# A decode-attention kernel that streams its caches: one load queue against two that take turns

## The chip, the cores and the metric

The kernel runs on one core of one Trainium2 chip. The metric is the device time of one execution in microseconds (us), the median over runs of the same kernel; lower is better.

## The reference

One token attends over two key/value caches of 8192 positions, and the two results are mixed by a gate. Block A has 16 heads with a cache each; block B has 16 query heads on 8 cached heads. Everything is float32, and a head has 256 numbers.

```python
def block(x, k_cache, v_cache, wq, wo, rep):            # A: rep 1, B: rep 2
    q = (x @ wq).reshape(1, 1, 16, 256).transpose(0, 2, 1, 3)
    k, v = repeat(k_cache, rep, axis=1), repeat(v_cache, rep, axis=1)
    p = softmax(einsum("bhqd,bhkd->bhqk", q, k) / 16)
    return einsum("bhqk,bhkd->bhqd", p, v).transpose(0, 2, 1, 3).reshape(1, 1, 4096) @ wo

g = sigmoid((x * gate_w).sum(-1, keepdims=True))
out = g * block(x, A_k, A_v, A_wq, A_wo, 1) + (1 - g) * block(x, B_k, B_v, B_wq, B_wo, 2)
```

## The kernel before, in words

All that is read (both caches, both wq and wo, x and the gate's weights) lies in one array, `stream`, in the order of use. The program works through 8 sets. A set has three units: two B heads that share a cache (unit 2), then A heads 0 and 1. A unit has 4 key tiles and 4 value tiles of 2 MB (128 partitions x 4096 numbers), so that a set has 12 of each; a value tile stands 3 tiles behind its key tile (`LEAD`).

`plan()` cuts the stream into `LOADS`, 54 **fills**, which I count from 0. Fills 0 to 50 hold 15872 numbers a partition (7936 KB; fill 0 has 8 more) and are one load each: almost four tiles, cut without regard to the tiles' ends. Fill 0 holds x, the gate's weights, the first wq and key tiles 0 to 2. Fills 51, 52 and 53 are cut into 2, 3 and 7 loads for the end of the program. That makes 63 loads.

Fills go in turn into the 3 slots of the pool `ring` (`SLOTS`). The loop at L464 takes a slot for the next fill, issues its loads on SyncE's queue (L469), and calls `piece` for each part of the fill (L472), which writes out the work on it. SyncE has nothing else to do: a load waits there until the engines are done with the fill that had the slot, three fills earlier, and then goes out.

What the work on a fill is, by lines:

- A key tile of unit 2 or of head 1 goes through `scores`: 16 matmuls on TensorE (L255), a minimum on VectorE (L261, L262), an exponential on ScalarE with its sum read by an accumulator read (L264), and a transpose on VectorE (L267).
- A key tile of head 0 goes through `scores_by_row` on VectorE: a multiply in place (L277) and a sum (L281) over the whole tile, some small steps, an exponential on ScalarE (L290) and a multiply (L294).
- A value tile goes through `attend`: 16 matmuls (L307). At a unit's end `take` (L316 on ScalarE, L317 on VectorE) copies the sum out, and `gather`, `combine` (L345 on ScalarE), `column` and `project_o` make the weights of the unit.
- wq goes through `project` (L220) and `spread`, wo through `emit_set` (L381) and, for the last set, `emit` (L398).

The order on each engine is the order in which the program is written (`manual_schedule`); the framework adds the waits.

Of the kernel before, what the change touches and what calls it, by code (L numbers as in the profile page):

```python
# [14 lines left out]
P = 128  # L15
# [18 lines left out]
SLOTS = 3  # L34
# [12 lines left out]
def plan():  # L47

    size = {"xg": XG, "k": ROWS * DH, "v": ROWS * DH, "wq": WQ, "wo": 8 * D}
    per = len(UNITS) * NT  # L50
    n = len(TILES)
    items = []
    for i in range(n + LEAD):
        if i == 0:
            items += [("xg", 0), ("wq", 0)]
        if i < n:
            items.append(("k", i))
        if i >= LEAD:
            items.append(("v", i - LEAD))
        if i % per == 7 and i // per + 1 < NS:  # L60
            items.append(("wq", i // per + 1))
        if i % per == LEAD + 1 and i >= per:
            items.append(("wo", i // per - 1))
    loads, room = [[]], FULL
    last = [("v", n - 3), ("v", n - 2)]
    for kind, i in items[:items.index(last[0])]:
        at, left = 0, size[kind]
        while left:
            step = min(left, room) // ATOM[kind] * ATOM[kind]
            if step:  # L70
                loads[-1].append((kind, i, at, step))
            at, left, room = at + step, left - step, room - step * (kind != "xg")
            if left:
                loads.append([])
                room = FULL

    loads = [[x] for x in loads]
    x = loads[-2][0]
    loads[-2] = [x[:2], x[2:]]
    loads[-1] += [[(kind, i, 0, size[kind])] for kind, i in last]  # L80
    at, end = 0, []
    for c in LAST_CUT:
        end.append([("v", n - 1, at, c * DH)])
        at += c * DH

    for h, e, n in ((3, 0, 2), (0, 0, 2), (1, 0, 3), (2, 1, 1)):
        end.append([("wo", NS - 1, (2 * h + e) * D, n * D)])
    return loads + [end]


LOADS = plan()
# [3 lines left out]
def kernel(  # L95
# [5 lines left out]
    nc = tc.nc  # L101
# [89 lines left out]
    def inputs(xs):  # L191
        nc.vector.tensor_copy(xz[:, :KF, 0], xs[:, :KF])
        nc.vector.tensor_copy(xz[:KR, KF, 0:1], xs[:KR, KF:])  # L193
        nc.vector.tensor_copy(xz[KR:, KF + 1, 0:1], xs[KR:, KF:])

    def prepare(gw):
        clear(YY[0], D)
        gp = ps_s.tile([1, 1], F32, name="sm")
        for c in range(KF + 1):
            nc.tensor.matmul(gp, xz[:, c, 0:1], gw[:, c:c + 1], start=(c == 0), stop=(c == KF))  # L200
        ge = const.tile([1, 1], F32, name="ge")
        nc.scalar.activation(ge, gp, AF.Exp, scale=-1.0)
        nc.vector.tensor_scalar(ge, ge, 1.0, None, op0=OP.add)
        nc.vector.reciprocal(gate[:, 0:1], ge)
        nc.vector.tensor_scalar(gate[:, 1:2], gate[:, 0:1], -1.0, 1.0, op0=OP.mult, op1=OP.add)
# [5 lines left out]
    def project(s, c0, w):  # L211

        if c0 == 0:
            QR[s] = ps_s.tile([2 * BLK, 2 * DH], F32, name="sm")
        q = QR[s]
        for j in range(w.shape[1]):
            a, c = divmod(c0 + j, KF)
            for a in (a,) if a < 2 else (0, 1):
                c = c if c0 + j < 2 * KF else KF
                nc.tensor.matmul(q[BLK * a:BLK * (a + 1), :], xz[:, c if c < KF else KF + a, :], w[:, j, :],  # L220
                                 start=(c == 0), stop=(c == KF), skip_group_check=True)
        if c0 + w.shape[1] == 2 * KF + 1:
            QR[s] = small.tile([P, NB * BLK], F32, name="px")[:2 * BLK, :2 * DH]
            nc.scalar.activation(QR[s], q, AF.Copy)

    def spread(s):

        qt = ps_s.tile([P, 2, 2, 2], F32, name="sm")
        qr = QR.pop(s)
        for h in range(2):  # L230
            for e in range(2):
                at = h * DH + e * P
                nc.tensor.matmul(qt[:, h, e, :], qr[:, at:at + P], rows4[:2 * BLK, :2], start=True, stop=True)
        for r, a, h, M in ((2, 0, 0, 2), (0, 1, 0, 1), (1, 1, 1, 1)):
            if (s, r) in BY_ROW:
                qa = ps_s.tile([P, DH], F32, name="sm")
                nc.tensor.matmul(qa, spread32, qr[:, h * DH:(h + 1) * DH], start=True, stop=True)  # L237
                QA[s, r] = small.tile([P, DH], F32, name="qa", bufs=1)
                nc.scalar.activation(QA[s, r], qa, AF.Copy, scale=-scale)
                continue  # L240
            nc.vector.tensor_scalar(QB[s % 2, r][:, :, BLK:BLK + M], qt[:, h:h + M, :, a].rearrange("p h e -> p e h"),
                                    -scale, None, op0=OP.mult)
# [76 lines left out]
    def gather(u):  # L319

        M = heads(u)
        GS[u] = small.tile([P, 2, NG, NT, M], F32, name=f"gs{M}")
        if u in BY_ROW:
            nc.vector.tensor_tensor(GS[u][:, :, :, :, 0], ST[u][:, :, None, :].to_broadcast([P, 2, NG, NT]),
                                    in4[:, :, :, None].to_broadcast([P, 2, NG, NT]), op=OP.mult)
            return
        pos = POS[M].rearrange("p g (t m) -> p g t m", m=M)
        for k in range(2):
            nc.vector.tensor_tensor(GS[u][:, k], ST[u][:, k, None, :, None].to_broadcast([P, NG, NT, M]), pos, op=OP.mult)
# [76 lines left out]
    def wait(n, f, *args):  # L406
        todo.append([n, f, args])

    def tick():
        for t in todo:  # L410
            t[0] -= 1
        for t in [t for t in todo if t[0] <= 0]:
            todo.remove(t)
            t[1](*t[2])

    def piece(kind, i, at, view):
        n = view.shape[-1] // ATOM[kind]
        j0 = at // ATOM[kind]
        if kind == "xg":
            inputs(view[:, :KF + 1])  # L420
            GW[0] = view[:, KF + 1:]
        elif kind == "wq":
            project(i, j0, view.rearrange("p (c n) -> p c n", c=n))
            if j0 + n < 2 * KF + 1:
                pass
            elif i == 0:
                spread(0)
                prepare(GW[0])
            else:
                wait(1, spread, i)  # L430
        elif kind == "k":
            u, t = TILES[i]
            if u in BY_ROW:
                scores_by_row(u, t, 2 * j0, view.rearrange("p (j d) -> p j d", d=DH))
            else:
                scores(u, t, j0, view.rearrange("p (c n) -> p c n", c=n))
            if j0 + n < 2 * NG:
                return
            tick()
            if t == NT - 1:  # L440
                gather(u)
                wait(1, combine, u)
                wait(2, column, u)
        elif kind == "v":
            u, t = TILES[i]
            n = view.shape[-1] // DH
            attend(u, t, at // DH, n, view.rearrange("p (j d) -> p j d", d=DH))
            if at // DH + n == ROWS:
                if t == NT - 1:
                    take(u)  # L450
                    if u != TILES[-1][0]:
                        wait(1, project_o, u)
                if i >= len(TILES) - LEAD:
                    tick()
        elif kind == "wo" and i < NS - 1:
            emit_set(i, j0, view.rearrange("p (c n) -> p c n", c=n))
            if i == NS - 2 and j0 + n == 8:
                fold()
        else:
            for j in range(n):  # L460
                LAST[divmod(j0 + j, 2)] = view[:, j * D:(j + 1) * D]

    off = 0
    for fill in LOADS:  # L464
        buf = ring.tile([P, FULL + XG], F32, name="slot")
        c = 0
        for load in fill:
            n = sum(x[3] for x in load)
            nc.sync.dma_start(buf[:, c:c + n], stream[off:off + P * n].rearrange("(p n) -> p n", p=P))  # L469
            off += P * n  # L470
            for x in load:
                piece(*x[:3], buf[:, c:c + x[3]])  # L472
                c += x[3]
    assert not todo
    s = NS - 1
    project_o((s, 1))
# [75 lines left out]
```

## Time and profile before

| | |
|---|---|
| median of 3 runs | 1010.63 us (1010.38 to 1011.29) |
| the profiled execution | 1010.95 us, span 1009.2 us |
| moved from memory | 432.02 MB, mean 429 GB/s over the span |
| busy share of the span: TensorE, VectorE, ScalarE | 57%, 46%, 9% |
| the loads' queue: share of the 16 DMA engines' span | 99.1% |
| granted TensorE clock, mean | 0.773 |

The profile is of one execution. Its span runs from the first instruction to the last; the execution's own time is 1.75 us longer than that. Busy time is the time in which an engine executes; a DMA engine's is the time that its packets took. For each idle stretch of an engine the profile names what ended it.

### The profile page before, as it was taken

The page shows a single profiled execution, that of the slowest core. Times are in us where ns is not written, and L with a number is a line of the kernel's source. Part 1 is how long each engine was busy: PE and PEld are TensorE (multiplying, and loading weights), DVE is VectorE, ACT ScalarE, POOL GpSimd, SP SyncE. Part 2 cuts the span into 40 slices and gives each one's busy share as a digit, 9 for nine tenths or more (in the row PEclk, how much of TensorE's full clock was granted, in tenths as well). Part 3 has the DMA queues.
Part 4 walks back from the last instruction along what each step waited for, and adds up shares of the span by engine and source line. Part 5 has one row for each costly group of instructions (what it writes and reads, how often), then busy time and mean ns, then how long its engine had stood idle before and what let it go on. Part 6 is the DMA issues. An engine that isn't in the chain of part 4 may idle for free.

```text
span 1009.2 us, 7624 instructions
## 1 busy us (share of the span) xinstructions
PE 578.0 (57%) x3154; PEld 169.8 (17%) x3154; DVE 465.1 (46%) x732; ACT 90.0 (9%) x267; POOL 1.9 (0%) x10
## 2 busy tenths in 40 slices
PE   0846745565745655636646556645656537537557
PEld 0211211121211111112111111111211112111112
DVE  1486213961248521576215841248521585216851
ACT  0100100010100110001100001100110000101010
POOL 0000000000000000000000000000000000000000
PEclk9977877767777887867787777776886777777788
DMA  9999999999999999999999999999999999999997
GB/s 403 439 438 425 431 436 439 435 421 433 439 436 425 436 431 441 431 428 433 441 428 429 438 431 433 435 431 438 431 431 426 440 438 426 428 433 441 424 421 299
DMA packets 9114, 432.50 MB, mean 429 GB/s; under 512 B 1016, under 2 KB 1144, under 8 KB 1784
## 3 DMA queue, kind: packets, MB, share of 16 engines
q1 hardware_dynamic: 9080, 432.02, 99.1%
q8 instruction: 24, 0.39, 0.2%
q14 instruction: 10, 0.08, 0.0%
HBM read 432.02 MB, written 0.00 MB: 428 GB/s over the span
## 4 chain that ended last, share of the span: by engine, by line
DMA 71%; PE 14%; DVE 12%; ACT 2%; issue 1%; ACTq 0%; SPq 0%; DVEq 0%
DMA slot<-in_stream_dram 71%; PE o L307 6%; PE sc L255 5%; DVE sr L281 4%; DVE slot L277 4%; PE sm L220 2%; ACT px L264 1%; DVE mn L261 1%; DVE pr L267 1%; PE sm L237 0%; DVE pr L294 0%; ACT pxr L290 0%; ACT ew L345 0%; PE sm L361 0%; DVE st L262 0%
## 5 line engine op out<-in xcount | busy, mean ns | idle before, releaser
L307 PE MATMUL o<-slot,pr 128*32 128x512 f32 (+1 forms) x1536 | 349.9, 758 | 224.6 <-DMA slot<-in_stream_dram 224.6
L255 PE MATMUL sc<-slot,qb 128*32 128x512 f32 x1024 | 197.5, 715 | 104.7 <-DMA slot<-in_stream_dram 101.7
L261 DVE TENSOR_REDUCE mn<-sc 128x1 f32<-128x512 f32 x64 | 44.1, 690 | 325.7 <-PE sc L255 300.9
L277 DVE TENSOR_TENSOR slot<-slot,qa 128x4096 f32<-128x4096 f32 (+7 forms) x40 | 142.6, 3565 | 41.1 <-DMA slot<-in_stream_dram 41.0
L307 PEld LDWEIGHTS o<-slot,pr 128*32 128x32 f32 (+1 forms) x1536 | 80.0, 142 | 405.2 <-DMA slot<-in_stream_dram 252.8
L281 DVE TENSOR_REDUCE sr<-slot 128x16 f32<-128x4096 f32 (+7 forms) x40 | 142.7, 3567 | 1.4
L255 PEld LDWEIGHTS sc<-slot,qb 128*32 128x32 f32 x1024 | 46.3, 129 | 221.1 <-issue 126.1
L264 ACT ACTIVATE px<-sc,st 128x512 f32<-128x512 f32 x64 | 44.0, 687 | 408.5 <-DVE st L262 386.6
L267 DVE STREAM_TRANSPOSE pr<-px 128x512 f32<-128x512 f32 x64 | 45.6, 713 | 58.9 <-ACT px L264 58.9
L220 PE MATMUL sm<-slot,xz 128*32 128x512 f32 x128 | 45.7, 707 | 35.8 <-DVE xz L193 23.0
L290 ACT ACTIVATE pxr<-sr,st 128x16 f32<-128x16 f32 x32 | 9.8, 308 | 373.6 <-DVE st L288 373.6
L372 PE MATMUL sm<-sel,ob 128*128 128x1 f32 (+1 forms) x96 | 17.5, 287 | 37.3 <-DVE ob L317 37.3
L317 DVE SCALAR_TENSOR_TENSOR ob<-o,half,ob 128x256 f32<-128x256 f32 x24 | 11.3, 470 | 44.0 <-ACT ob L316 44.0
L372 PEld LDWEIGHTS sm<-sel,ob 128*128 128x128 f32 x96 | 15.5, 228 | 61.8 <-DVE ob L317 53.6
L220 PEld LDWEIGHTS sm<-slot,xz 128*32 128x32 f32 x128 | 11.1, 128 | 65.4 <-issue 27.8
L294 DVE TENSOR_TENSOR pr<-pxr,cols 128x256 f32<-128x256 f32 x32 | 13.6, 426 | 15.9 <-ACT pxr L290 15.9
L316 ACT ACTIVATE ob<-o,half 128x256 f32<-128x256 f32 x24 | 11.3, 469 | 49.5 <-PE o L307 49.5
L361 PE MATMUL sm<-ones,wr 1*128 1x1 f32 x48 | 9.7, 268 | 10.4 <-DVE wr L354 10.4
L237 PE MATMUL sm<-px,spread 64*128 64x256 f32 x16 | 6.6, 498 | 13.9 <-DVE es L347 13.9
L381 PE MATMUL Y<-slot,ocs 128*1 128x448 f32 x112 | 13.4, 595 | 0.0
L361 PEld LDWEIGHTS sm<-ones,wr 1*128 1x128 f32 x48 | 7.8, 203 | 32.8 <-issue 28.1
L264 ACT ACTIVATION_READ_ACCUMULATOR px<-sc,st 128x1 f32 x64 | 12.3, 193 | 0.0
(73 smaller groups left out, 142.4 us busy)
## 6 DMA issues: line engine op xcount, KB each, us to landing
slot<-in_stream_dram SPq DMA_DIRECT2D x50, 7936.0 KB, 42.6
slot<-in_stream_dram SPq DMA_DIRECT2D x1, 7940.0 KB, 22.0
slot<-in_stream_dram SPq DMA_DIRECT2D x1, 4864.0 KB, 41.0
slot<-in_stream_dram SPq DMA_DIRECT2D x2, 2048.0 KB, 25.3
slot<-in_stream_dram SPq DMA_DIRECT2D x1, 3072.0 KB, 29.9
slot<-in_stream_dram SPq DMA_DIRECT2D x1, 1280.0 KB, 20.8
slot<-in_stream_dram SPq DMA_DIRECT2D x1, 1024.0 KB, 24.2
slot<-in_stream_dram SPq DMA_DIRECT2D x2, 512.0 KB, 25.5
```

The source lines that it names most:

```text
L220: nc.tensor.matmul(q[BLK * a:BLK * (a + 1), :], xz[:, c if c < KF else KF + a, :], w[:, j, :], start=(c == 0), stop=(c == KF), skip_group_ ...
L255: nc.tensor.matmul(sc[32 * g:32 * (g + 1), :], qb[:, e, at:at + 32], kt[:, j, :], start=(e == 0), stop=(e == 1), skip_group_check=True)
L261: nc.vector.tensor_reduce(mn, sc, axis=AX.X, op=OP.min)
L264: nc.scalar.activation(px, sc, AF.Exp, bias=st[:, 0, t:t + 1], scale=-1.0, accum_out=st[:, 1, t:t + 1])
L267: nc.vector.transpose(pr.rearrange("p (q r k) -> p q k r", r=BLK, k=2), px.rearrange("p (q k c) -> p q k c", c=BLK, k=2))
L277: nc.vector.tensor_tensor(kt, kt, QA[u][:, None, :].to_broadcast([P, n, DH]), op=OP.mult)
L281: nc.vector.tensor_reduce(sc[:, j0:j0 + n], kt, axis=AX.X, op=OP.add)
L294: nc.vector.tensor_tensor(pr, px[:, :, None, :].to_broadcast([P, ROWS // 2, NG * NT, 2]), cols[:, t].rearrange("p g r -> p (g r)")[:, None ...
L307: nc.tensor.matmul(O[u][w * g:w * (g + 1), :], pr[:, j // 2, :w], vt[:, j - j0:j - j0 + 2, :], start=(t == 0 and j < 2 * P // w), stop=(t ...
L361: nc.tensor.matmul(cl, WR.pop(u).rearrange("p c x m k -> p (c x m k)"), ones[:1, :], start=True, stop=True)
L372: nc.tensor.matmul(oc[:, e, :M], OB[u][:, e::2], SEL[u][:, :M], start=True, stop=True)
L381: nc.tensor.matmul(YY[0][32 * h:32 * h + 1, :], OC[s, r][:, e, m:m + 1], wt[:, j, :], start=False, stop=(s == NS - 2 and e == 1), skip_gro ...
```

## The change

The loads are taken out of the loop into `ask(k)`, which takes the slot for fill k and issues its loads. Fills with an even number go out on SyncE's queue, fills with an odd one on ScalarE's; the last three all go out on SyncE's. The first three fills are asked for ahead of the loop. In the loop, fill k + 3 is asked for behind the work on fill k. On SyncE that is the place that it had. On ScalarE, whose instructions run in the order in which they are written, the load now stands among the exponentials and copies: behind all that ScalarE has to do for fill k.

```diff
-    off = 0
-    for fill in LOADS:
+    off = [0]
+    queues = [nc.sync, nc.scalar]
+
+    def ask(k):
         buf = ring.tile([P, FULL + XG], F32, name="slot")
         c = 0
+        for load in LOADS[k]:
+            n = sum(x[3] for x in load)
+
+            queue = queues[k % 2 if k < len(LOADS) - 3 else 0]
+            queue.dma_start(buf[:, c:c + n], stream[off[0]:off[0] + P * n].rearrange("(p n) -> p n", p=P))
+            off[0] += P * n
+            c += n
+        return buf
+
+    bufs = [ask(k) for k in range(SLOTS)]
+    for k, fill in enumerate(LOADS):
+        c = 0
         for load in fill:
-            n = sum(x[3] for x in load)
-            nc.sync.dma_start(buf[:, c:c + n], stream[off:off + P * n].rearrange("(p n) -> p n", p=P))
-            off += P * n
             for x in load:
-                piece(*x[:3], buf[:, c:c + x[3]])
+                piece(*x[:3], bufs[k][:, c:c + x[3]])
                 c += x[3]
+        if k + SLOTS < len(LOADS):
+            bufs.append(ask(k + SLOTS))
```

On ScalarE, at the program's start, the difference reads as follows (`slot` is a ring slot, `sc` the scores of a key tile, `px` their exponentials; `-` is before, `+` the change):

```order
+L474 DMA slot<-in_stream_dram 128x15872
 L224 ACT_TABLE_LOAD
 L224 ACTIVATE px<-sm 64x512
 L239 ACTIVATE qa<-sm 128x256
 L202 ACTIVATE ge<-sm 1x1
-L264 ACTIVATE px,st<-sc,st 128x512 x4
+L264 ACTIVATE px,st<-sc,st 128x512 x3
+L474 DMA slot<-in_stream_dram 128x15872
+L264 ACTIVATE px,st<-sc,st 128x512
```

The first DMA is fill 1, the second fill 3. Fill 3 stands behind the exponentials of the three key tiles of fill 0, whose slot it takes.

On SyncE the changed program has these loads at its start (with the semaphores that each waits for; the DMAHW ones are landings of earlier fills):

```order
L474 DMA slot<-in_stream_dram 128x15880
L474 DMA slot<-in_stream_dram 128x15872
L474 DMA slot<-in_stream_dram 128x15872 [waits DMAHW1_49,DVE_49,PE_49]
L474 DMA slot<-in_stream_dram 128x15872 [waits DMAHW0_49,DMAHW3_49,DVE_49,PE_49]
L474 DMA slot<-in_stream_dram 128x15872 [waits DMAHW5_49,DMAHW2_49,PE_49]
```

These are fills 0, 2, 4, 6 and 8. Before, fills 0 to 53 stood there one behind the other. Now SyncE has 26 of the whole fills (0, 2, ..., 50) and all loads of the last three, and ScalarE has 25 (1, 3, ..., 49).

## Rows read from the trace of the kernel before

**Rows 1.** The page: the DMA engines in 40 slices, the queues, the share of the chain.

```profile
DMA  9999999999999999999999999999999999999997
GB/s 403 439 438 425 431 436 439 435 421 433 439 436 425 436 431 441 431 428 433 441 428 429 438 431 433 435 431 438 431 431 426 440 438 426 428 433 441 424 421 299
...
q1 hardware_dynamic: 9080, 432.02, 99.1%
...
DMA 71%; PE 14%; DVE 12%; ACT 2%; issue 1%; ACTq 0%; SPq 0%; DVEq 0%
```

**Rows 2.** Windows: one long stretch and five of the end (last columns: granted clock, DMA share, GB/s).

```profile
core 0: us, PE busy (x) PEld busy (x) DVE busy (x) ACT busy (x) POOL busy (x), PEclk, DMA share, GB/s
5.00:980.00 975.00, 559.30 (x2982) 163.49 (x2982) 456.94 (x692) 86.73 (x261) 0.00 (x0) 0.77 1.00 433
975.00:980.00 5.00, 1.62 (x16) 0.26 (x8) 1.57 (x4) 0.78 (x2) 0.00 (x0) 1.00 0.97 419
980.00:985.00 5.00, 2.07 (x12) 0.59 (x16) 0.00 (x0) 0.00 (x0) 0.00 (x0) 0.61 0.98 419
985.00:990.00 5.00, 5.00 (x36) 1.47 (x32) 1.34 (x3) 0.47 (x1) 0.00 (x0) 0.71 1.00 425
990.00:995.00 5.00, 3.17 (x34) 0.89 (x26) 2.02 (x10) 1.04 (x3) 0.00 (x0) 1.00 0.98 404
995.00:1000.00 5.00, 3.69 (x28) 1.01 (x30) 0.16 (x1) 0.00 (x0) 0.00 (x0) 1.00 0.96 385
```

**Rows 3.** The page's DMA issues: the whole fills, median us from issue to landing.

```profile
slot<-in_stream_dram SPq DMA_DIRECT2D x50, 7936.0 KB, 42.6
```

**Rows 4.** Timeline of the first 64 us: start, us, engine, line, what (idle before, and what ended it).

```profile
0.74 55.66 SPq L469 DMA_DIRECT2D slot<-in_stream_dram  x5
...
22.82 0.17 DVE L192 COPY xz<-slot 128x3 f32<-128x3 f32 x1 [16.79 <-DMA slot<-in_stream_dram]
...
40.80 0.69 ACT L264 ACTIVATE px<-sc,st 128x512 f32<-128x512 f32 x1 [1.63 <-DVE st L262]
41.39 0.19 ACT L264 ACTIVATION_READ_ACCUMULATOR px<-sc,st 128x1 f32 x1
...
41.57 2.90 PE L255 MATMUL sc<-slot,qb 128*32 128x512 f32 x16 [2.83 <-ACT px L264]
...
60.57 4.42 DVE L277 TENSOR_TENSOR slot<-slot,qa 128x4096 f32<-128x4096 f32 x1 [0.97 <-DMA slot<-in_stream_dram]
```

**Rows 5.** Timeline of SyncE's queue, 37 to 40 us: fill 3 is issued.

```profile
38.80 0.33 SPq L469 DMA_DIRECT2D slot<-in_stream_dram  x1
```

**Rows 6.** DMA queues, 46.8 to 48 us: packets, MB, share of 16 engines in these 1.2 us.

```profile
q1 hardware_dynamic: 15, 0.95, 185.6%
q8 instruction: 1, 0.02, 5.1%
```

**Rows 7.** Timeline, ScalarE's last step for fill 14, and SyncE's issue of fill 17.

```profile
303.48 0.33 SPq L469 DMA_DIRECT2D slot<-in_stream_dram  x1
...
305.22 0.42 ACT L345 ACTIVATE ew<-sm,mnr 1x16 f32<-1x16 f32 x2 [0.70 <-DVE mnr L343]
```

**Rows 8.** Timeline: issue and first use of fill 12, and of fill 45.

```profile
214.67 0.33 SPq L469 DMA_DIRECT2D slot<-in_stream_dram  x1
...
249.19 1.08 PE L255 MATMUL sc<-slot,qb 128*32 128x512 f32 x4 [11.28 <-DMA slot<-in_stream_dram]
...
834.86 0.33 SPq L469 DMA_DIRECT2D slot<-in_stream_dram  x1
...
870.43 1.93 PE L307 MATMUL o<-slot,pr 128*32 128x512 f32 x8 [8.88 <-DMA slot<-in_stream_dram]
```

**Rows 9.** DMA queues, 100 to 900 us (large packets), then 992 to 997 us (small ones).

```profile
q1 hardware_dynamic: 6122, 346.01, 100.0%
...
q1 hardware_dynamic: 375, 2.01, 98.4%
```

**Rows 10.** Timeline: SyncE issues the first load of fill 53, and the last work.

```profile
974.11 0.33 SPq L469 DMA_DIRECT2D slot<-in_stream_dram  x1
...
1004.76 1.55 PE L398 MATMUL Y<-slot,ocs 128*1 128x112 f32 x32 [0.19 <-DMA slot<-in_stream_dram]
...
1006.67 0.66 SPq L484 DMA_DIRECT2D out_dram<-ys  x1
```

## The prediction

> **What bounds the kernel now.** I read the page first: the slices, the queues and the chain of waits. The DMA engines are nine tenths busy or more in all slices but the last, the loads' queue fills 99.1% of 16 engines' span, and 71% of the chain that ended last is DMA [rows 1]. So the loads bound the kernel, and the first question is whether the engines ever pause. In the windows they do not: from 5 to 980 us the DMA share is 1.00 at 433 GB/s [rows 2]. At that pace the 432.02 MB take 997.7 us of the 1009.2 us span. The other 11.5 us are the first landing, the smaller loads of the end (385 to 425 GB/s in the last windows [rows 2]), and the last matmuls and the store behind the last landing at 1004.8 us [rows 10]. A change to the loads can gain only if it raises the pace. It can lose wherever the engines run dry.
>
> How far are they from that? A whole fill is 8.126 MB (7936 KB), 18.77 us at 433 GB/s. It takes 42.6 us from issue to landing in the median [rows 3], so it spends most of that time queued behind others. That is the reserve. The smallest that I found are at fill 12 (issued at 214.67, first used at 249.19: 34.5 us) and fill 45 (834.86 to 870.43: 35.6 us) [rows 8]. A fill that finds the queue empty needs 22.08 us from issue to first use (fill 0: 0.74 to 22.82 [rows 4]). So the reserve there is 34.5 - 22.1 = 12.4 us, and 13.5 us.
>
> **The change, part by part.**
>
> *The order of the bytes.* With one queue the fills go one after another. With two, what matters is whether a DMA engine serves two queues at once. The trace of before has one case: fetches of instructions come on another queue than the loads. From 46.8 to 48 us one such packet of 16 KB has 5.1% of 16 engines' 1.2 us, that is 0.98 us, beside 15 packets of the loads [rows 6]. One engine's share of 433 GB/s is 27.1 GB/s, at which 16 KB alone take 0.60 us. So it neither waited for the loads' packets to end nor stopped them: it shared. I take it that fills on two queues share too, in equal parts. [...]
>
> *The start.* Fills 0 and 1 go out at the same time, now on two queues. Sharing, both land when the second lands now. Before, fill 0 is first used at 22.82, fill 1 at 41.57, fill 2 at 60.57 [rows 4]. So fill 0 is used from about 41.6, up to 18.8 us later, and nothing else is outstanding then but fill 2, which lands at about 60.5 as before. Fill 3 has to be asked for soon enough to follow it. Before, that is at 38.80 [rows 5], 16.0 us behind the first use of fill 0. Now it stands on ScalarE behind the third exponential of fill 0. That starts at 40.80, and its accumulator read ends at 41.58 [rows 4]: 18.0 to 18.8 us behind the first use. So fill 3 is asked for at 41.57 + 18.0 = 59.6, at the latest at 60.3. It finds an empty queue and is usable 22.08 us later, at 81.6 to 82.4. Without a pause it would be usable at 60.57 + 18.77 = 79.3. **The hole is 2.3 to 3.1 us wide**, and since no bandwidth is spare later, it goes to the end in full. Its lower bound is nothing: should the two fills take turns row by row, fill 0 lands a row earlier (18.77 / 8 = 2.3 us), and part of the 22.08 us may be a cold start. I take 2.3 us, the nearer end of the rows.
>
> *Loads behind ScalarE's work.* There are 24 more loads on ScalarE, less fill 3: 23. Each waits for the later of the slot's release and ScalarE's step ahead of it. At fill 17 that is the two small exponentials at 305.22 to 305.64, where the load went out at 303.48: 2.2 us late [rows 7]. This and fill 3 are the worst that I found; at the others ScalarE has mostly been done before the release. These delays come out of the reserve and cost nothing while it lasts. The other way round, a load that waits for its slot holds up the exponentials behind it. They need scores of the next fill, which TensorE makes only behind its work on this one, so I put that at nothing; should one be held, it comes out of the same reserve. The issue itself is 0.33 us [rows 5], 25 times on ScalarE: 8 us on an engine that is busy 86.73 of 975 us [rows 2].
>
> *The reserve from then on.* With two fills sharing, one lands every 18.77 us still, but at each landing the next one is half done instead of not begun, and the one behind it has taken that half. Work on a fill so begins up to half a fill, 9.4 us, later against the bytes moved, and the slot comes free as much later. The reserve shrinks from 12.4 to 3.0 us at fill 12 and from 13.5 to 4.1 us at fill 45. ScalarE's delays there are below that. I put this at nothing; upper bound below.
>
> *The end.* The last three fills are on one queue and in order, so their bytes land in order. Behind fill 50 the engines are then up to 9.4 us late. From 975 to 1000 us TensorE is busy 1.62 + 2.07 + 5.00 + 3.17 + 3.69 = 15.55 of 25 us [rows 2]: 9.45 us are idle, just enough to catch up. Fill 53, asked for at 974.11 [rows 10], would go out at some 984 us, with over 15 us of loads still ahead of it. I put the end at 0.2 us, between 0 and 1.
>
> *The pace.* The same 16 engines, the same rows: nothing.
>
> **The sum.** 1010.95 (the profiled execution's own time) + 2.3 + 0.2 = 1013.45 us. That execution lies 0.32 us above the median of the runs, so **1013.1 us** for the median. For this case alone the range is 1010.8 to 1014.8.
>
> **The rivals.** A measurement of this kernel can tell about 0.2%, 2.0 us, from no change: below 1008.6 is faster, above 1012.65 slower.
>
> *A: the fills do not share.* If each engine sends its 8 rows of one fill before it turns to the other queue, fill 0 lands at 22.8 as before, fill 3 goes out in time, and the reserve stays at 12 us. Then the time is that of before, 1010.6 us. [...] Against it: the shared fetch. 0.15.
>
> *B: two queues raise the pace.* Place: between an engine's packets. From 100 to 900 us 6122 packets with 346.01 MB took 100.0% of 12800 us of engine time; from 992 to 997 us 375 packets with 2.01 MB took 98.4% of 80 us [rows 9]. Two unknowns, a time for each packet and one for each MB, give 12.8 ns for each packet. All 9080 packets [rows 1] have so 116 us on 16 engines, 7.3 us each. If a second queue's data fill these, the time is 1013.1 - 7.3 = 1005.8 us. It decides from the point at which more than 4.5 us of the 7.3 are hidden, or 2.0 us without the hole. For it: the engines' pace is constant, so a small cost for each packet would show wherever it is hidden. Against it: nothing in this trace has two queues of loads at once. [...] 0.17.
>
> *C: the small reserve gives out.* In every set VectorE's head-0 tiles make late releases like those of fills 12 and 45. If the reserve of 3 to 4 us is missed by 2 us at two of the eight, the time is 1013.1 + 4 = 1017 us; by 1 us at all eight, 1021 us. For it: 3 us is less than what ScalarE's delay and a different TensorE clock could take. Against it: the delays at those fills are small. 0.13.
>
> *D: two queues lower the pace.* If each row is slower beside another, the bound is the lowest slice, 421 GB/s [rows 1]: 432.02 MB take 28.5 us more there. The shared fetch shows no such loss [rows 6]. 0.07.
>
> **How the numbers follow.** The forecast has 0.48. Of it, 0.30 lies above 1012.65 (the hole is over 2.0 us) and 0.18 within 0.2%. A is within 0.2% with 0.15. Of B, 0.13 is faster and 0.04 within 0.2%. C and D are slower, 0.20. So faster 0.13, the same 0.37, slower 0.50. The range leaves out D, the far end of C and the best part of B: 1007.5 to 1017.0 us.
>
> **What the profile after would show.** Right: two queues with about half of the bytes each; the first use of fill 0 at about 41 us instead of 22.8; a slice or window near 60 us in which the DMA share falls below 1, for some 2 us, and none later; a median from issue to landing still near 40 us; the last work some 2.5 us later than now. Fill 0 at 22.8 us would say A. More than 433 GB/s from 100 to 900 us would say B, less D, and dips near the head-0 tiles C. I am wrong if the time is below 1010.8 or above 1014.8 us, and about the mechanism if fill 0 lands early.

## The result, and the profile after

The changed kernel takes 1012.39 us in the median (1011.40 to 1013.60, 19 runs), the kernel before 1010.58 us (1010.32 to 1011.76, 19 runs). The ratio is 1.0018, with a 95% interval of 1.0011 to 1.0024: 1.8 us slower, between 1.1 and 2.4. That is just inside the 0.2% that I had called "the same", and 0.7 us below the 1013.1 us that I gave. The profiled execution took 1012.23 us, its span 1010.4 us.

The slices, queues and issues of the page after (compare [rows 1, 3]):

```profile
DMA  9999999999999999999999999999999999999997
GB/s 402 442 403 435 423 430 440 438 430 423 435 435 435 432 433 430 433 435 428 438 433 435 430 426 442 438 425 430 433 440 433 431 427 418 437 438 440 420 419 324
...
q1 hardware_dynamic: 5480, 228.86, 52.5%
q10 hardware_dynamic: 3600, 203.16, 46.6%
...
slot<-in_stream_dram ACTq DMA_DIRECT2D x25, 7936.0 KB, 41.2
slot<-in_stream_dram SPq DMA_DIRECT2D x25, 7936.0 KB, 42.6
slot<-in_stream_dram SPq DMA_DIRECT2D x1, 7940.0 KB, 40.1
```

There are two queues with about half of the bytes each. The shares of the 16 engines' time still add up to 99.1%, as with one queue: packets of the two queues did not overlap on an engine, they took turns. How large a turn is, three windows of 2.3 us show, about as long as one row of 62 KB takes (`--dma --window` 33.6:35.9, 36.0:38.3, 38.4:40.7):

```profile
q1 hardware_dynamic: 16, 1.02, 102.0%
...
q10 hardware_dynamic: 16, 1.02, 101.9%
...
q1 hardware_dynamic: 32, 1.02, 102.2%
q10 hardware_dynamic: 16, 0.00, 0.4%
```

In these windows the 16 engines take a row each from q1 (SyncE), then a row each from q10 (ScalarE). In the third window are also 16 packets of 4 bytes of each queue: the ends of fills 0 and 1. Fill 0 (the 7940 KB) lands 40.1 us after its issue, where a load that had the engines to itself (fill 0 before) was used after 22.1 us. The third slice, 50 to 76 us, has 403 GB/s where it had 438.

The timeline at the start after (compare [rows 4, 5]; ACTq and SPq are the queues of ScalarE and SyncE):

```profile
40.94 0.17 DVE L192 COPY xz<-slot 128x3 f32<-128x3 f32 x1 [34.91 <-DMA slot<-in_stream_dram]
...
58.37 0.69 ACT L264 ACTIVATE px<-sc,st 128x512 f32<-128x512 f32 x1 [1.63 <-DVE st L262]
58.42 0.33 ACTq L474 DMA_DIRECT2D slot<-in_stream_dram  x1
...
71.35 0.33 SPq L474 DMA_DIRECT2D slot<-in_stream_dram  x1
...
95.01 0.33 ACTq L474 DMA_DIRECT2D slot<-in_stream_dram  x1
```

Fill 0 is used 18.1 us later than before. Fill 3 goes out at 58.42, fill 4 at 71.35, fill 5 at 95.01.

Where bytes were lost can be read from windows only roughly. A window counts a packet where it starts, and one of 62 KB lasts 2.3 us at an engine's 27.1 GB/s, so a window of a few us swings by itself, and one of 80 us still by up to some 5 GB/s. First before (last columns: granted clock, DMA share, GB/s):

```profile
45.00:125.00 80.00, 52.08 (x246) 16.20 (x246) 49.66 (x63) 7.90 (x25) 0.00 (x0) 0.76 1.00 431
440.00:500.00 60.00, 34.18 (x185) 10.46 (x183) 31.97 (x40) 5.43 (x17) 0.00 (x0) 0.73 1.01 435
500.00:800.00 300.00, 175.12 (x938) 50.31 (x930) 129.27 (x206) 26.70 (x79) 0.00 (x0) 0.76 1.00 433
800.00:900.00 100.00, 57.98 (x334) 17.30 (x332) 49.48 (x78) 8.91 (x28) 0.00 (x0) 0.79 1.00 431
```

and the same windows after:

```profile
45.00:125.00 80.00, 51.14 (x285) 16.26 (x281) 52.06 (x71) 9.44 (x29) 0.00 (x0) 0.85 0.99 420
440.00:500.00 60.00, 32.03 (x174) 10.38 (x166) 35.75 (x46) 4.37 (x15) 0.00 (x0) 0.80 1.00 434
500.00:800.00 300.00, 176.37 (x952) 50.59 (x952) 125.82 (x204) 27.81 (x81) 0.00 (x0) 0.74 1.00 433
800.00:900.00 100.00, 51.94 (x279) 16.08 (x278) 52.94 (x79) 8.15 (x26) 0.00 (x0) 0.77 1.00 431
```

In these windows only the first differs clearly. A finer reading is a **count** from the packets of the trace: with each packet's bytes spread over the time that it took, one has the moment at which a kernel had moved a given number of bytes, and the difference between two kernels' moments is how far one is behind the other. Two kernels with one queue that come below (everything on ScalarE, and late loads on one queue) stay within 0.1 us of the kernel before, all the way to 984 us.

By the count the changed kernel is 0.2 us ahead at 57 us and then falls behind at four places: by 1.4 us at fill 3 (57 to 94 us), 0.5 us at fill 5 (94 to 130), 0.3 us at fill 12 (200 to 250) and 0.8 us at fill 45 (830 to 856). At 984 us it is 2.8 us behind. The window from 800 to 900 us does not show the last of these. The issue of fill 45 after, and a narrower window, before and after, do:

```profile
847.97 0.33 ACTq L474 DMA_DIRECT2D slot<-in_stream_dram  x1
```

```profile
845.00:852.00 7.00, 2.19 (x10) 0.64 (x14) 1.83 (x9) 0.94 (x4) 0.00 (x0) 0.71 1.01 435
845.00:852.00 7.00, 6.39 (x26) 2.27 (x28) 6.93 (x6) 0.03 (x1) 0.00 (x0) 0.55 0.94 383
```

Not all of the 2.8 us is left at the end. The last matmuls after (compare [rows 10]) start 1.9 us later than before and take 0.95 instead of 1.55 us, and the store goes out at 1007.95 instead of 1006.67, 1.3 us later:

```profile
1006.64 0.95 PE L398 MATMUL Y<-slot,ocs 128*1 128x112 f32 x32 [0.18 <-DMA slot<-in_stream_dram]
```

### The profile page after: what moved, and what is told of

Read it like the earlier page. It is cut to its first block, busy times and chain, and to the rows that moved or that the text cites. A ratio compares the mean times of both kernels' runs of the same rounds, so it can differ in the third digit from the quotient of the medians.

```text
span 1010.4 us, 7638 instructions
## 1 busy us (share of the span) xinstructions
PE 562.4 (56%) x3154; PEld 167.8 (17%) x3154; DVE 464.5 (46%) x732; ACT 89.8 (9%) x267; POOL 1.9 (0%) x10
## 3 DMA queue, kind: packets, MB, share of 16 engines
q1 hardware_dynamic: 5480, 228.86, 52.5%
q10 hardware_dynamic: 3600, 203.16, 46.6%
## 4 chain that ended last, share of the span: by engine, by line
DMA 62%; DVE 23%; PE 11%; ACT 2%; issue 2%; another core or an unknown queue 1%; ACTq 0%; DVEq 0%; SPq 0%
DMA slot<-in_stream_dram 62%; DVE slot L277 9%; DVE sr L281 9%; PE o L307 5%; PE sc L255 4%; PE sm L220 1%; ACT px L264 1%; DVE pr L294 1%; DVE mn L261 1%; ACT pxr L290 1%; DVE pr L267 1%; DVE mt L287 0%; DVE st L288 0%; PE sm L372 0%
## 5 line engine op out<-in xcount | busy, mean ns | idle before, releaser
L307 PE MATMUL o<-slot,pr 128*32 128x512 f32 (+1 forms) x1536 | 338.5, 751 | 204.0 <-DMA slot<-in_stream_dram 204.0
L255 PE MATMUL sc<-slot,qb 128*32 128x512 f32 x1024 | 185.8, 707 | 99.8 <-DMA slot<-in_stream_dram 99.2
L372 PE MATMUL sm<-sel,ob 128*128 128x1 f32 (+1 forms) x96 | 18.1, 292 | 51.0 <-DVE ob L317 51.0
## 6 DMA issues: line engine op xcount, KB each, us to landing
slot<-in_stream_dram SPq DMA_DIRECT2D x1, 7940.0 KB, 40.1
slot<-in_stream_dram SPq DMA_DIRECT2D x1, 1024.0 KB, 15.8
```

Of the source, the lines that this page charges most:

```text
L255: nc.tensor.matmul(sc[32 * g:32 * (g + 1), :], qb[:, e, at:at + 32], kt[:, j, :], start=(e == 0), stop=(e == 1), skip_group_check=True)
L307: nc.tensor.matmul(O[u][w * g:w * (g + 1), :], pr[:, j // 2, :w], vt[:, j - j0:j - j0 + 2, :], start=(t == 0 and j < 2 * P // w), stop=(t ...
L372: nc.tensor.matmul(oc[:, e, :M], OB[u][:, e::2], SEL[u][:, :M], start=True, stop=True)
```

## The experiments

Medians here stand against runs of the kernel before on the same chip (1010.55 to 1010.86 us). The count is of one execution of each kernel; a table at the end has it for all that fell behind.

**First three fills in order.** `queue = queues[k % 2 if SLOTS <= k < len(LOADS) - 3 else 0]`

> Fills 0, 1 and 2 all on SyncE's queue, turns from fill 3 on. Theory (the loss is made at the start, because fill 0 shares the engines with fill 1 and its slot comes free 18 us later): first use of fill 0 at about 22.8 us again, no pause of the DMA engines near 60 us, 1010.5 to 1011.2 us; a dip near fill 45 (848 us) may stay. Rival 1 (turns cost pace, all along): 1012.0 to 1012.6. Rival 2 (the dips near the head-0 tiles make the loss): 1012.0 to 1012.6.

Measured: 1015.25 us, ratio 1.0043 (1.0029 to 1.0056). All three expectations of the time missed. Its timeline:

```profile
40.39 0.38 ACTq L474 DMA_DIRECT2D slot<-in_stream_dram  x1
...
77.96 4.43 DVE L277 TENSOR_TENSOR slot<-slot,qa 128x4096 f32<-128x4096 f32 x1 [17.92 <-DMA slot<-in_stream_dram]
...
98.20 0.34 ACTq L474 DMA_DIRECT2D slot<-in_stream_dram  x1
```

and its window:

```profile
45.00:125.00 80.00, 38.79 (x192) 12.16 (x192) 47.21 (x57) 6.07 (x20) 0.00 (x0) 0.74 0.96 409
```

Fill 0 was used at 22.65 us again, and nothing paused near 60 us. But fill 3, asked for at 40.39, now shared with fill 2, which was used at 77.96 instead of 60.57. So fill 5 was asked for at 98.20, and by the count 3.6 us were lost there and 1.2 us at fill 12. The loss was not at the start as such: it had moved to where the turns begin.

**Fill 3 on SyncE.** `queue = queues[k % 2 if k != 3 and k < len(LOADS) - 3 else 0]`

> As the change, but fill 3 alone goes to SyncE's queue, so that it no longer stands behind ScalarE's third exponential. Fill 0 still shares and is first used at about 41 us. Theory: fill 3 is asked for when its slot comes free, 2.0 us earlier (about 56.4), ahead of the landing of fill 2 at 59 to 59.6; no pause near 60 us; 1010.6 to 1011.3 us. Rival (what costs is the late start of the work, 18 us, wherever fill 3 is asked for): 1012.0 to 1012.6.

Measured: 1012.68 us, ratio 1.0022 (1.0012 to 1.0033). Missed. The timeline, fill 3 and then fill 5:

```profile
56.74 0.33 SPq L474 DMA_DIRECT2D slot<-in_stream_dram  x1
...
95.37 0.34 ACTq L474 DMA_DIRECT2D slot<-in_stream_dram  x1
```

and the window:

```profile
45.00:125.00 80.00, 51.26 (x287) 16.53 (x283) 52.06 (x71) 9.42 (x29) 0.00 (x0) 0.85 0.99 421
```

Fill 3 went out 1.7 us earlier. The window is much like that of the change (420), but the count tells the places apart: 0.4 us were lost at fill 3 instead of 1.4, 0.9 at fill 5, asked for at 95.4, instead of 0.5, 0.8 at fill 12 instead of 0.3, and nothing at fill 45. So ScalarE's delay did make most of the pause at fill 3, as the theory had it. But the time did not fall: most of what was saved there was lost at the fills that were late next.

**Everything on ScalarE.** `queue = queues[1 if k < len(LOADS) - 3 else 0]`

> Fills 0 to 50 all on ScalarE's queue, the last three on SyncE's: the place among ScalarE's instructions without the sharing. Theory (the place alone costs nothing while one queue keeps a reserve of 12 us): fill 0 first used at about 22.8 us, no pauses, 1010.2 to 1011.2 us. Rival (loads behind ScalarE's work are late and cost time by themselves): 1012 us or more.

Measured: 1010.73 us, ratio 1.0003 (0.9994 to 1.0011); 433 GB/s from 45 to 125 us. As expected: loads that stand among ScalarE's instructions cost nothing on one queue.

**The turns swapped.** `queue = queues[1 - k % 2 if k < len(LOADS) - 4 else 0]`

> Even fills on ScalarE's queue, odd ones on SyncE's, the last four on SyncE's: so fill 3 and fill 45, at which the changed kernel's engines ran dry, are asked for by SyncE. Theory: fill 0 still used at about 41 us, fill 3 asked for at about 56.4 us, no pause near 60 us; the late places move to even fills, which have more reserve; 1010.6 to 1011.4 us. Rival (sharing as such costs pace): 1012.0 to 1012.6.

Measured: 1012.63 us, ratio 1.0020 (1.0011 to 1.0029). Missed. It has 425 against 431 GB/s from 45 to 125 us and 422 against 430 from 205 to 255 us; by the count that is 1.0 us at fills 3 and 5, 1.3 at fill 12, and none at fill 45. Which fills stand on which engine changes the places, and the time little.

That made a new theory: what turns take away is the **reserve**, everywhere, and the loss comes out wherever the work asks for a load just too late. Rival: turns cost something fixed for each load.

**Late loads, with turns and without.** Ahead of the odd fills' loads from fill 3 on, twelve idle copies; once as in the change, once with fills 0 to 50 all on ScalarE's queue:

```diff
+    dum = const.tile([P, 2, 256], F32, name="dum")
+    nc.vector.memset(dum, 0.0)
+
+    def idle(n):
+        for _ in range(n):
+            nc.scalar.activation(dum[:, 1, :], dum[:, 0, :], AF.Copy)
...
+        if k % 2 == 0 and k + SLOTS < len(LOADS) - 3:
+            idle(12)
         if k + SLOTS < len(LOADS):
             bufs.append(ask(k + SLOTS))
```

> As the change, but twelve idle copies of 256 numbers (some 0.4 us each, 5 us in all) stand on ScalarE ahead of each of its loads from fill 3 on. Theory (with turns the engines have 0 to 4 us of reserve at several fills, so a late load goes to the end): fill 3 is asked for at about 63.3 us, 5 us late, fill 5 about 4 us late, and at each set's head-0 tiles something is lost; 1017 us or more. Rival (the reserve is ample and what turns cost is a fixed loss at a few loads): fill 3 alone goes to the end, 1016 to 1017.5 us, and no further pauses.

> Fills 0 to 50 on ScalarE's queue alone, with the same twelve idle copies ahead of the odd ones. Theory: with one queue the reserve is 12 us at its smallest, so loads that are up to 5 us late cost nothing; 1010.4 to 1011.3 us. Rival (late loads cost as such): as much over 1010.6 as the same copies add to the change.

Measured: with turns 1025.20 us, ratio 1.0141 (1.0127 to 1.0154); on one queue 1010.67 us, ratio 1.0001 (0.9992 to 1.0010). First with turns, the timeline and then the windows:

```profile
59.45 5.33 ACT L484 ACTIVATE dum<-dum 128x256 f32<-128x256 f32 x12
64.37 0.34 ACTq L474 DMA_DIRECT2D slot<-in_stream_dram  x1
```

```profile
45.00:125.00 80.00, 49.69 (x255) 15.81 (x255) 50.55 (x67) 18.41 (x51) 0.00 (x0) 0.79 0.90 382
440.00:500.00 60.00, 42.83 (x204) 13.61 (x207) 45.69 (x54) 10.65 (x32) 0.00 (x0) 0.76 0.99 426
500.00:800.00 300.00, 154.97 (x899) 48.10 (x889) 122.31 (x199) 63.94 (x171) 0.00 (x0) 0.74 0.99 425
```

then the same on one queue:

```profile
41.71 5.33 ACT L484 ACTIVATE dum<-dum 128x256 f32<-128x256 f32 x12
46.63 0.33 ACTq L474 DMA_DIRECT2D slot<-in_stream_dram  x1
```

```profile
45.00:125.00 80.00, 49.63 (x242) 15.29 (x242) 49.60 (x63) 19.10 (x53) 0.00 (x0) 0.76 1.00 431
500.00:800.00 300.00, 174.18 (x927) 50.17 (x926) 128.97 (x205) 65.77 (x174) 0.00 (x0) 0.75 1.00 433
```

With turns and the copies, 5.3 us each time, the kernel is 14.6 us slower than the kernel before and 12.8 us slower than the changed kernel; on one queue the same copies cost nothing. The windows account for it: 49, 9 and 8 GB/s below those of before are 9.1 + 1.2 + 5.5 = 15.8 us; the count has 16.1. More was lost than fill 3's 5 us, and in several places. The rival falls.

**Half-sized fills.** `FULL = 7936`, `SLOTS = 6`, the last value tiles as fills of their own; on one queue, and in turns with the last six on SyncE's.

> Fills of half the size in six slots, all on SyncE's queue; the last fills in other cuts. A control for the next kernel: the same bytes in order, 1009.5 to 1012 us. No pauses.

> Fills of half the size in six slots, in turns, the last six on SyncE's queue. Theory (what turns take from the reserve is half a fill, and a pair of first fills lands late by one fill): both are halved, fill 0 is used at about 22 us, and the loss over the same cuts on one queue falls to 0 to 0.8 us. Rival (each load that starts beside the other queue costs time): twice as many loads, 2 to 4 us over the same cuts on one queue.

Measured: one queue 1014.51 us, ratio 1.0037 (1.0025 to 1.0050); turns 1014.82 us, ratio 1.0044 (1.0030 to 1.0058). The control lay above the band that I had given it. The first row is its load queue, the other two are those of the kernel with turns:

```profile
q1 hardware_dynamic: 16856, 432.03, 99.3%
```

```profile
q1 hardware_dynamic: 9368, 227.65, 52.4%
q10 hardware_dynamic: 7488, 204.38, 46.9%
```

Turns cost 0.3 us here, less than the runs can tell, though there are twice as many loads; fill 0 was used at 21.6 us, and by the count neither kernel has a pause. The rival falls, and the theory that what turns take from the reserve goes with the size of a fill fits. The control itself is 3.9 us over the kernel before with 16856 instead of 9080 packets, which is 3.9 x 16 / 7776 = 8.0 ns for each further packet. It falls behind evenly (431 against 433 GB/s from 100 to 900 us; by the count 1.9 us at 440 us and 4.0 at 984), so the other cuts of its end are not what costs.

**The same turns, begun two fills apart.** `queue = queues[k % 2 if 21 <= k < len(LOADS) - 3 else 0]`, and with 23 for 21.

> Fills 0 to 20 on SyncE's queue, turns from fill 21 on. Theory: the first fill that goes to the second queue shares with the one ahead of it and overtakes none of the work it needs, but the fill already queued behind lands late; what that costs depends on the work then due. Adding up the fills' times from landing to release in the trace of before, with two queues that share equally, I get no pause here, and the least reserve at fill 45, 1.2 us: 1010.5 to 1011.5 us. Rival (turns cost a little at each load): 1011.5 to 1012 us, and the next kernel within 0.3 us of this one.

> Fills 0 to 22 on SyncE's queue, turns from fill 23 on: two fills later than the kernel before this one. Theory: the same sum gives a pause of 5.0 us near 471 us, where fill 25 is asked for behind the head-0 tiles: 1014.5 to 1017 us, with the DMA engines dry near 471 us. Rival (turns cost a little at each load): within 0.3 us of turns from fill 21.

Measured: from 21 on 1010.66 us, ratio 0.9998 (0.9990 to 1.0007); from 23 on 1015.15 us, ratio 1.0046 (1.0032 to 1.0060). The windows from 21 on:

```profile
440.00:500.00 60.00, 33.78 (x162) 10.86 (x162) 35.79 (x48) 4.66 (x16) 0.00 (x0) 0.70 1.01 435
500.00:800.00 300.00, 172.91 (x952) 49.48 (x952) 126.37 (x207) 27.89 (x81) 0.00 (x0) 0.77 1.00 433
```

the issue of fill 45 in that kernel, and a window around it:

```profile
846.22 0.33 ACTq L474 DMA_DIRECT2D slot<-in_stream_dram  x1
```

```profile
840.00:855.00 15.00, 10.68 (x55) 3.65 (x55) 13.39 (x17) 1.64 (x6) 0.00 (x0) 0.73 0.94 395
```

and from 23 on, first the timeline with the first use of fill 22 and the issue of fill 25, then the windows:

```profile
456.21 8.46 PE L307 MATMUL o<-slot,pr 128*64 128x512 f32 x32 [19.81 <-DMA slot<-in_stream_dram]
...
475.56 0.33 ACTq L474 DMA_DIRECT2D slot<-in_stream_dram  x1
```

```profile
440.00:500.00 60.00, 29.06 (x160) 9.52 (x160) 33.28 (x37) 4.25 (x14) 0.00 (x0) 0.73 0.93 394
500.00:800.00 300.00, 166.28 (x942) 49.01 (x942) 124.34 (x201) 27.00 (x79) 0.00 (x0) 0.76 1.00 433
```

Both times are as expected. Fill 23, alone on the new queue, delays fill 22, which TensorE waits 19.81 us for and uses at 456.21; VectorE's head-0 work follows, fill 25 is asked for at 475.56, and by the count 5.3 us are lost, where the sum had 5.0. Begun two fills earlier, the delayed fill has less work on it (10 us from its landing to the next load into its slot, against 19), and over half of the program in turns takes no time that can be measured. One thing is not as expected: from 21 on the engines did pause, at fill 45, where the sum left 1.2 us. By the count 1.0 us was lost there (395 GB/s in the window, against 432 before), but the time shows none of it.

Where the engines fell behind the kernel before, by the count (us; the stretches are in the time of the kernel before), and what the medians show:

| kernel | fill 3 (57 to 94) | fill 5 (94 to 130) | 200 to 250 | 250 to 830 | fill 45 (830 to 856) | behind at 984 | median over before |
|---|---|---|---|---|---|---|---|
| the change | 1.4 | 0.5 | 0.3 | 0.0 | 0.8 | 2.8 | 1.8 |
| first three in order | 0.0 | 3.6 | 1.2 | 0.0 | 0.0 | 4.9 | 4.7 |
| fill 3 on SyncE | 0.4 | 0.9 | 0.8 | 0.0 | 0.0 | 1.9 | 2.1 |
| turns swapped | 0.9 | 0.1 | 1.3 | 0.0 | 0.0 | 2.2 | 2.1 |
| late loads, turns | 7.4 | 2.3 | 1.0 | 5.6 | 0.0 | 16.1 | 14.6 |
| turns from 21 on | 0.0 | 0.0 | 0.0 | 0.0 | 1.0 | 1.0 | -0.2 |
| turns from 23 on | 0.0 | 0.0 | 0.0 | 5.2 | 0.1 | 5.3 | 4.3 |

## Why the prediction was right

*The bound and the sign.* Right: the loads bound the kernel, no bandwidth is spare, and a pause goes to the end. But not in full: the pauses at fills 3, 5 and 12 leave the kernel 2.1 us behind, the one at fill 45 makes it 2.8, and the result is 1.8 us. Where fill 45's pause stands alone, with turns from fill 21 on, the time shows none of its 1.0 us. The changed kernel's trace has part of the loss made up in the last loads and matmuls; why, no run shows.

*Sharing.* Right in effect: both first fills land at about 40 us. In form it was the lower bound's picture, rows in turn, and what I had drawn from that came true for the data alone: the last rows of fill 0 ended between 37.5 and 38.2 us, a row ahead of those of fill 1. But a load ends with 16 packets of 4 bytes (25 fills on q10 have 3600 packets, 144 each: 128 rows and these 16). Those of fill 0 went out from 39.87 us on, each as the other queue's row ended, so fill 0 landed with fill 1 and not a row earlier. Rival A, whole fills one after another, falls: the engines took turns, but a turn was one row here (2.3 us in the three windows above) and not an engine's 8 rows of a fill.

*The start, "the hole is 2.3 to 3.1 us wide".* The step held in place, but the hole was 1.4 us wide. Fill 3 went out 0.05 us after the third exponential's start, not after its accumulator read, and at 58.42 instead of 59.6, since fill 0 was used 0.6 us earlier than I had it and the work on it took 17.4 instead of 18.0 us. With 58.42 the step's own sum gives 58.42 + 22.08 - 79.34 = 1.2 us. I had put everything behind fill 3 at nothing, and that step failed: 0.5 us more was lost at fill 5, 0.3 at fill 12 and 0.8 at fill 45. Fills 0 to 4 are all that is asked for ahead of fill 5; their 5 x 18.77 = 93.9 us of bytes end at about 97 us, counted from the first bytes some 3 us into the span. Fill 5 can go out only when the work on fills 0, 1 and 2 is done, which starts at 40.9 and ends at 95. Those two times nearly meet, and a load can take 3.3 us more than its transfer (fill 0 before: 22.08 - 18.77) to be usable. Taking the pause out at fill 3 only brings the engines to fill 5 sooner. Where fill 5 went out at 98.2 the loss there was 3.6 us. That the time came out within 0.7 us is in part luck: a hole that I had 0.9 us too wide stood in for 0.8 us at fills 5 and 12, and the 0.8 us at fill 45, which I had missed too, did not show in the time.

*The reserve from then on, "I put this at nothing".* Wrong, in a small way, at the two fills that I had named: I left 3.0 us at fill 12 and 4.1 at fill 45, and there 0.3 and 0.8 us were lost. Fill 45 was asked for 13.1 us later than before (847.97 against 834.86); 2.1 us of that are the earlier pauses, so 11.0 us are left where I had 9.4. And I had reckoned from landings, when the last engine is done: by the packets an engine had nothing left at 847.8 us, while the last row of fill 44 ended at 852.7. This is rival C's mechanism at a fraction of its price. With 5 us more delay it gets rival C's size and more, where one queue does not notice.

*Loads behind ScalarE's work* at nothing: right, shown by the kernel with all of them there. *The end* at 0.2 us: not measured by itself; by the count nothing is lost from 856 to 984 us, and behind that the changed kernel makes up some of what it had lost. *The pace* at nothing: right. Rival B falls: with twice as many packets and two queues the time was not below that of one queue. Its 12.8 ns for a packet measured 8.0 ns. Rival D falls with 433 GB/s in both kernels.

## What to carry to other kernels

Where one queue kept all DMA engines busy, a second one moved no more bytes (433 GB/s from 100 to 900 us with either); it delivered two loads side by side, the one ahead later (fill 0 landed 40.1 us after its issue instead of 22.0), and with a fixed number of slots the reserve shrank by part of a load (11.0 of 18.77 us at fill 45). Before spreading loads, compare the time from issue to landing with the bare transfer, and look at which work the delayed load would hold up. When a pause is found, ask what would be late next: here most of what was saved at fill 3 was lost again at fills 5 and 12. And read small losses from the packets, not from windows that count a packet where it starts.

## What the runs showed of the hardware that was not expected

Packets of two queues of loads ran in turn, in the windows from 33.6 to 40.7 us one row of 62 KB at a time, not side by side: the shares of the queues' time add up to one (52.5 and 46.6%), although a 16 KB fetch beside the loads before took 0.98 us [rows 6], where an engine's 27.1 GB/s would give 0.60. The two first fills landed within 0.2 us of each other, as the issues in the first microsecond show:

```profile
slot<-in_stream_dram SPq DMA_DIRECT2D x1, 7940.0 KB, 40.1
slot<-in_stream_dram ACTq DMA_DIRECT2D x1, 7936.0 KB, 40.3
```

The first rows behind the pause at fill 3 were slow: these 16 are all that was moved from 59 to 62 us, and took 102.7% of 16 engines' 3 us, 3.1 us each instead of 2.3.

```profile
q10 hardware_dynamic: 16, 1.02, 102.7%
```

Halving the packets' size at the same bytes cost 3.9 us, some 8 ns for each further packet of a stream that keeps the engines busy.
